# Attention with a gated convolution: periodic due times, row sums inverted in 128 rows, the last keys turned by VectorE, the low parts of the weights made by TensorE

## The chip, the cores and the metric

The kernel runs on one core of one Trainium2 chip. The metric is the device time of one execution in microseconds (us). The core has TensorE (PE; PEld is its weight load), VectorE (DVE), ScalarE (ACT), GpSimd (POOL) and SyncE (SP), which here only issues DMAs.

## The reference: what is computed

Inputs are q, k, v of shape (8 batches, 8 heads, 576 positions, 64), two 512x512 matrices `w_val` and `w_out`, and 5 convolution taps for each of 512 channels, these three as 64-bit floats.

```python
scores = scale * np.matmul(q_rot, k_rot.transpose(0, 1, 3, 2))
attn = np.exp(scores - np.max(scores, axis=-1, keepdims=True))
attn = attn / (np.sum(attn, axis=-1, keepdims=True) + 1e-09)
x = heads_joined(np.matmul(attn, v))            # (8, 576, 512)
gate_pre += conv_w[k][None, None, :] * xp[:, k:k + S, :]   # k = 0..4, causal
out = (1.0 / (1.0 + np.exp(-gate_pre)) * (x @ w_val)) @ w_out
```

`q_rot` and `k_rot` are q and k with rotary position embedding.

## The kernel before

**Pairs.** Two heads are worked on together, so there are 32 pairs (`p`), four to a batch. For a pair, q and k lie with 64 channels of each head on 128 partitions. One pair goes through these steps (names as in the code):

- `load`, `rope_mul`, `rope_add`, `qk_hi`, `qk_lo`: q and k come by DMA into one buffer each (`qin`, `kin`), are rotated, and split into a rounded high part (ACT) and a low part. Every score is the sum of three fp32r products, high x high, high x low, low x high.
- `s_mm`, `s_max`, `s_exp`: the 576 queries are taken in four chunks of 128 for each head, and the last 64 queries of both heads together (chunk 4). A chunk of 128 queries by 576 keys fills one of three PSUM tiles `ps_s`. DVE finds its maximum (L275), ACT takes the exponential (L288) and adds up the rows into a column of `sums`.
- Turning: for the product with v the keys must lie on partitions. For the first `EARLY` pairs and the last, TensorE transposes blocks of 128x128 through the identity (L318) into a bank of `ps_t`, of which there are two, and ACT or DVE copies it to `big` (`t_copy`). For all others, DVE transposes blocks of 32x32 (`turn`, L304) and 16 DMAs (`move`, L309) carry the blocks to their partitions. In both cases the last 64 keys of both heads are turned apart by TensorE (`th_mm`, L332, four transposes a pair) and copied to `pl` by ACT (`h_copy`).
- Sums: `hm_mm` turns the pair's nine columns of sums by TensorE into 16x128 (L362), `r_inv` adds 1e-9 and takes the reciprocal on DVE (L398, L399), `r_write` stores them in DRAM, and `r_read` reads them back, spread over 64 partitions.
- `pv_mm`, `pvm_mm`, `x_norm`, `xm_norm`: product with v, times the inverted sums.
- `x_hi`, `x_lo`, `tap`, `gate`: the result is split in high and low, and convolved (L446, four instructions on DVE, one on ACT).

After four pairs a batch is complete: `f_mm` (L472) multiplies by `w_val`, `y_mul`, `y_hi`, `y_lo` apply the gate and split, and `f_mm` multiplies by `w_out`; 16 groups of 12 matmuls a batch, dealt out between the matmuls of later pairs.

**Weights.** `load_weight` brings a 128x512 block of 64-bit numbers; DVE takes them apart with integer and float steps (`decode`, L506 to L512), ACT rounds to the high part (L517), and DVE subtracts it and adds the rest for the low part (L518, L519). There are eight blocks, all decoded during the first pairs.

**What sets the order.** Every step is a job with an engine, a cost, a due time (18 us times the pair, plus an offset, plus a number from the table `DUE`) and tokens that say what it reads and writes. `Plan.order` plays the jobs through with these costs: on each engine it starts, of the jobs that could begin within a short span, the one due first. What comes out is the order of instructions on each engine; engines then run in that order and wait for each other by semaphores. `PICK` says for jobs that several engines could do which one does them ('V' is DVE, 'A' ACT, 'G' POOL). SP's order is that of the DMAs, and a DMA that waits holds up all behind it.

## Time and profile before

| | |
|---|---|
| time, median of 3 runs | 727.49 us (727.17 to 730.32) |
| the profiled execution | 730.04 us, its span 728.2 us |
| TensorE clock granted, mean | 0.972 |
| PE busy | 653.0 us, 90% |
| DVE busy | 630.7 us, 87% |
| ACT busy | 464.7 us, 64% |
| POOL busy | 423.3 us, 58% |
| DMA queue of SP | 64.8% of 16 engines, 128.15 MB |

A matmul of fp32 operands shows as two instructions. The reciprocal of a pair's sums (L399) is a good mark of time, since there is one a pair: the one of pair 5 starts at 159.23 us, the one of pair 31 (the last) at 684.75 us. So the execution has an early stretch (0 to 159 us, with the weights), 26 steady pairs, and an end of 43 us.

### The profile page before, as it was taken

What the parts mean: (1) busy time and instruction counts of PE and PEld (TensorE: products, weight loads), DVE (VectorE), ACT (ScalarE), POOL (GpSimd) and SP (SyncE); (2) the same over time, 40 slices, a digit from 0 to 9 for tenths busy, and PEclk for the clock granted to TensorE, in tenths of its full rate; (3) what the DMA queues carried; (4) which work ended last, traced back from release to release, by engine and by line L of the source; (5) the groups of instructions that cost most, each with busy time, mean ns of one, the idle gap of its engine ahead of it and who ended that gap; (6) DMA issues with size and microseconds to landing.
All of it is one profiled execution on the core that took longest, in us unless ns stands there. A gap on an engine that the chain in (4) does not pass through costs nothing.

```text
span 728.2 us, 14173 instructions
## 1 busy us (share of the span) xinstructions
PE 653.0 (90%) x5044; PEld 473.2 (65%) x5044; DVE 630.7 (87%) x980; ACT 464.7 (64%) x1125; POOL 423.3 (58%) x312
## 2 busy tenths in 40 slices
PE   2787865799999989999899999999999899999998
PEld 2554552666666766777666666777665676777597
DVE  6999989999989998998889997889889899898452
ACT  3676564576776667676486666676686667776431
POOL 4474347278568775876657655777757555781000
PEclk9999878799999999999999999999999999999999
DMA  7245133558888787877976877878876868866101
GB/s 257 66 130 186 30 101 129 114 154 220 231 226 217 206 214 195 214 213 216 225 205 186 211 203 184 213 202 214 232 222 175 221 184 222 215 187 153 49 33 66
DMA packets 52245, 129.63 MB, mean 178 GB/s; under 512 B 11184, under 2 KB 21200, under 8 KB 52176
## 3 DMA queue, kind: packets, MB, share of 16 engines
q1 hardware_dynamic: 51632, 128.15, 64.8%
q8 instruction: 40, 0.66, 0.4%
q10 hardware_dynamic: 544, 0.59, 0.3%
q14 instruction: 29, 0.24, 0.1%
HBM read 62.48 MB, written 9.59 MB: 99 GB/s over the span
## 4 chain that ended last, share of the span: by engine, by line
PE 37%; DVE 31%; DMA 13%; ACT 6%; SPq 6%; issue 5%; POOL 2%; DVEq 0%; ACTq 0%; POOLq 0%
PE ps_t L472 13%; PE ps_t L377 9%; DVE nm L275 9%; PE ps_s L269 8%; DVE g L446 6%; DVE big L304 6%; SPq L309 4%; DMA kin<-in_k 4%; ACT p L288 3%; DMA v<-in_v 3%; DMA big<-big 3%; PE ps_t L380 3%; DMA rb<-rd 2%; DVE kin L233 2%; DVE rr L399 1%
## 5 line engine op out<-in xcount | busy, mean ns | idle before, releaser
L288 ACT ACTIVATE p<-ps_s,nm 128x576 f32<-128x576 f32 x256 | 188.1, 739 | 79.1 <-DVE nm L275 76.6
L275 DVE TENSOR_REDUCE nm<-ps_s 128x1 f32<-128x576 f32 x288 | 204.2, 738 | 23.4 <-PE ps_s L269 22.4
L269 PE MATMUL ps_s<-k,q 64*128 64x288 f32 x1536 | 152.0, 320 | 20.2 <-ACT k L244 8.9
L269 PEld LDWEIGHTS ps_s<-k,q 64*128 64x128 f32 x1536 | 116.6, 193 | 52.2 <-issue 21.0
L304 DVE STREAM_TRANSPOSE big<-p 128x512 f32<-128x512 f32 x216 | 142.4, 685 | 6.1 <-ACT p L288 5.9
L233 POOL TENSOR_TENSOR qin<-qin,tab 128x576 f32<-128x576 f32 x59 | 87.5, 1497 | 70.4 <-DMA qin<-in_q 64.3
L446 DVE SCALAR_TENSOR_TENSOR g<-x,cw,g 128x576 f32<-128x576 f32 (+1 forms) x132 | 125.6, 956 | 1.9 <-ACT g L443 1.7
L377 PE MATMUL ps_t<-big,v 128*64 128x512 f32 (+2 forms) x528 | 119.4, 586 | 5.5 <-DMA rd<-rr 3.2
L472 PE MATMUL ps_t<-yh,wout_hi 128*128 128x288 f32 x256 | 81.2, 317 | 4.9 <-ACT pl L213 1.8
L472 PE MATMUL ps_t<-xh,wval_hi 128*128 128x288 f32 x256 | 80.1, 313 | 3.1 <-DVE g L477 2.0
L237 POOL TENSOR_TENSOR kin<-kin 128x576 f32<-128x576 f32 (+1 forms) x32 | 51.0, 1594 | 45.9 <-DVE kin L233 38.8
L472 PE MATMUL ps_t<-yh,wout_lo 128*128 128x288 f32 x256 | 77.5, 303 | 0.0
L472 PE MATMUL ps_t<-yl,wout_hi 128*128 128x288 f32 x256 | 77.4, 302 | 0.0
L472 PE MATMUL ps_t<-xl,wval_hi 128*128 128x288 f32 x256 | 76.8, 300 | 0.0
L472 PE MATMUL ps_t<-xh,wval_lo 128*128 128x288 f32 x256 | 76.5, 299 | 0.0
L377 PEld LDWEIGHTS ps_t<-big,v 128*64 128x64 f32 x528 | 36.1, 136 | 62.1 <-issue 56.4
L433 POOL TENSOR_TENSOR xl<-x,xh 128x576 fp32r<-128x576 f32 (+1 forms) x32 | 51.5, 1608 | 41.6 <-ACT xh L429 39.9
L485 POOL TENSOR_TENSOR yl<-g,yh 128x288 fp32r<-128x288 f32 x56 | 47.2, 843 | 34.9 <-ACT yh L481 34.8
L248 POOL TENSOR_TENSOR q<-qin,q 128x576 fp32r<-128x576 f32 (+1 forms) x32 | 49.2, 1536 | 31.3 <-ACT q L244 31.3
L233 POOL TENSOR_TENSOR kin<-kin,tab 128x576 f32<-128x576 f32 x34 | 52.5, 1547 | 14.5 <-DMA kin<-in_k 14.5
L248 POOL TENSOR_TENSOR k<-kin,k 128x576 fp32r<-128x576 f32 x31 | 45.8, 1479 | 23.0 <-ACT k L244 21.9
L472 PEld LDWEIGHTS ps_t<-yh,wout_hi 128*128 128x128 f32 x256 | 49.2, 192 | 10.4 <-DVE g L477 2.6
(86 smaller groups left out, 1150.5 us busy)
## 6 DMA issues: line engine op xcount, KB each, us to landing
big<-big SPq DMA_DIRECT2D x432, 128.0 KB
kin<-in_k SPq DMA_DIRECT2D x31, 576.0 KB
qin<-in_q SPq DMA_DIRECT2D x31, 576.0 KB
v<-in_v SPq DMA_DIRECT2D x32, 320.0 KB
rb<-rd SPq DMA_DIRECT2D x64, 144.0 KB
out_t<-oo SPq DMA_DIRECT2D x64, 144.0 KB
big<-in_w_val SPq DMA_DIRECT2D x4, 512.0 KB
big<-in_w_out SPq DMA_DIRECT2D x4, 512.0 KB
```

The source lines that it names most:

```text
L233: eng.tensor_tensor(out=t[:, i, a:b], in0=t[:, i, a:b], in1=tabs[:, i, a:b], op=ALU.mult)
L237: eng.tensor_tensor(out=t[:, 0], in0=t[:, 0], in1=t[:, 1], op=ALU.add)
L248: eng.tensor_tensor(out=t[:, 1], in0=ins[n][:, 0, a:b], in1=t[:, 0].bitcast(F32), op=ALU.subtract)
L269: T.matmul(out=ps[:, half, 0:288], lhsT=st["q"][rows, x, c * 128:c * 128 + 128] if c < 4 else mixq[p % 2][:, x], rhs=st["k"][rows, y, k0:k ...
L275: V.tensor_reduce(out=st[f"nm{i}"], in_=st[f"s{i}"], axis=AX.XY, op=ALU.max, negate=True)
L288: A.activation(out=pd.rearrange("p (b x) -> p b x", b=2), in_=st[f"s{i}"], func=AF.Exp, bias=st[f"nm{i}"], scale=1.0, accum_out=sums[p % 2 ...
L304: V.transpose(out=t[:, :, cs.index(c), h].rearrange("p b k i -> p k b i"), in_=st[f"p{c}"][:, h, h * D:h * D + M].rearrange("p (k b i) -> ...
L377: T.matmul(out=acc[HEAD[h], 0:n], lhsT=st["v"][:, j, h, :], rhs=st["pt"][:, :, c0:c1, h, j].rearrange("p a c i -> p c a i"), start=(j == 0 ...
L433: eng.tensor_tensor(out=st["xl"][:, a:b], in0=xs[p % 2][:, 4 + a:4 + b], in1=st["xh"][:, a:b].bitcast(F32), op=ALU.subtract)
L446: V.scalar_tensor_tensor(out=g, in0=x_sb[:, a + k:b + k], scalar=w, in1=g, op0=ALU.mult, op1=ALU.add)
L472: T.matmul(out=acc[:, 0:n], lhsT=wt[w][:, kc, ds], rhs=mv, start=(kc == 0 and i == 0), stop=(kc == NCH - 1 and i == 2))
L485: eng.tensor_tensor(out=ffn[b, "l", dc, lo], in0=y, in1=ffn[b, "h", dc, lo].bitcast(F32), op=ALU.subtract)
```

## The change

- **Order.** `Plan.order` no longer plays costs through. It takes, among all jobs whose forerunners have been placed and whose buffers can be given, always the one due first. The due times have 18.5 us times the pair, and a new table `DUE` (the offset of `exp0`, for instance, goes from -341.33 to -875.49); `PICK` is new too. For the pairs after the early ones, `rope_mul` of k's first half goes from DVE to POOL (`kmul0` 'V' to 'G'), `hm_copy` from ACT to DVE (`chm`), and one in four `o_out` from ACT to DVE (`od1`). For the early pairs, POOL gives three rope steps of k to DVE and takes two of q.
- **Early pairs.** `EARLY` goes from 4 to 5: pair 4 is turned by TensorE.
- **Sums.** `r_inv` works on the sums as they lie, 9 columns in 128 rows, and writes them beside the exponentials of chunk 4 in `pm`, so that the transpose of the last 64 keys of `pm` turns them too. The transpose L362 is gone, and `r_write` now follows the copy `hm_copy`.
- **Last keys.** For pairs turned by DVE, `turn` of the second head takes five blocks of 128 keys and the other four, so that all 9 x 128 columns are turned; `th_mm` and `h_copy` remain for pairs turned by TensorE. Each `move` carries 144 KB and not 128 KB. `pl` is gone.
- **Weights.** One mask step of `decode` becomes an Abs on ACT; the subtraction and addition on DVE become three matmuls of 512 columns through the identity and its negative (`w_mm`) and a copy by ACT (`w_low`).
- Of the buffers `yh` and `yl` there are 7 and not 8.

```diff
-EARLY = 4
+EARLY = 5
...
-            "rb": 2, "rr": 1, "yl": 8, "oo": 3, "rd": 2, "ps_s": 3, "ps_t": 2, "nm": 4}
+    BUFS = {"p": 3, "pm": 1, "big": 3, "pq": 1, "xh": 5, "xl": 5, "g": 5, "yh": 7, "rb": 2, "yl": 7, "oo": 3, "rd": 2,
+            "ps_s": 3, "ps_t": 2, "nm": 4}
...
+        heap = [(jobs[i][0], i) for i in range(len(jobs)) if not left[i]]
+        heapify(heap)
         done = []
+        while heap:
+            i = heappop(heap)[1]
...
+                done.append(i)
+                for o in outs[i]:
+                    left[o] -= 1
+                    if not left[o]:
+                        heappush(heap, (jobs[o][0], o))
...
+        k0, k1 = ((0, 4), (4, 9))[h]
+        V.transpose(out=t[:, :, cs.index(c), k0:k1].rearrange("p b k i -> p k b i"),
+                    in_=st[f"p{c}"].rearrange("p h s -> p (h s)")[:, k0 * 128:k1 * 128].rearrange("p (k b i) -> p k b i", b=4, i=32))
...
-        T.transpose(out=st["bhm"][:, 0:128], in_=st["pm"][:, 448:S], identity=ident)
-        T.transpose(out=st["bhm"][0:16, 128:256], in_=sums[p % 2], identity=ident)
+        T.transpose(out=state[p]["bhm"][:, 0:128], in_=pm[:, M:S + D], identity=ident)
...
-        V.tensor_scalar(out=r, in0=st["bhm"][0:16, 128:256], scalar1=1e-9, scalar2=None, op0=ALU.add)
-        V.reciprocal(out=r, in_=r)
+        r = sums[p % 2][:, 0:9]
+        V.tensor_scalar(out=r, in0=r, scalar1=1e-9, scalar2=None, op0=ALU.add)
+        V.reciprocal(out=pm[:, S:S + 9], in_=r)
...
-            lambda: V.tensor_scalar(out=hi, in0=hi, scalar1=0x7FF00000, scalar2=None, op0=ALU.bitwise_and),
+            lambda: A.activation(out=fh, in_=fh, func=AF.Abs) if whole is None else
+            V.tensor_scalar(out=hi, in0=hi, scalar1=0x7FF00000, scalar2=None, op0=ALU.bitwise_and),
...
-            lambda: eng.tensor_tensor(out=fa, in0=fa, in1=hi_out.bitcast(F32), op=ALU.subtract),
-            lambda: eng.tensor_tensor(out=lo_out, in0=fa, in1=fh, op=ALU.add),
...
+    def w_mm(n, c):
+        _, fa, fh = wsteps[n, c]
+        b = wstage["lo", n, c] = bank(f"ps_t/w{n}{c}")
+        T.matmul(out=b, lhsT=minus, rhs=w_hi[n][:, c], start=True, stop=False)
+        T.matmul(out=b, lhsT=ident, rhs=fa, start=False, stop=False)
+        T.matmul(out=b, lhsT=ident, rhs=fh, start=False, stop=True)
+
+    def w_low(n, c, eng):
+        cast(eng, w_lo[n][:, c], wstage["lo", n, c])
```

**How the order moves.** First PE in pair 0: between the scores of chunks 1 and 3. Before (L269 are scores, L318 and L332 transposes of the exponentials `p`):

```order
L269 MATMUL ps_s_163<-k_70,q_72 128x288
L318 MATMUL ps_t_178<-ident,p_158 128x128 x4
L318 MATMUL ps_t_188<-ident,p_158 128x128 x4
L269 MATMUL ps_s_201<-k_70,q_72 128x288
L269 MATMUL ps_s_202<-k_70,q_72 128x288
```

With the change (L230 are scores, L280 a transpose, L506 to L508 the new matmuls for the first block of `w_val`):

```order
L230 MATMUL ps_s_193<-k_71,q_73 128x288
L280 MATMUL ps_t_206<-ident,p_190 128x128 x4
L506 MATMUL ps_t_220<-wval_hi,minus 128x512
L507 MATMUL ps_t_220<-big_118,ident 128x512
L508 MATMUL ps_t_220<-big_118,ident 128x512
L230 MATMUL ps_s_228<-k_71,q_73 128x288
L230 MATMUL ps_s_229<-k_71,q_73 128x288
```

The scores of chunk 3 now stand behind matmuls that need a decoded block.

Second, POOL in a steady pair. `qin`, `kin` are the two input buffers; L233 is `rope_mul`, L237 `rope_add`, L248 `qk_lo`, L433 `x_lo`. Before:

```order
L233 TENSOR_TENSOR kin<-kin,tab 128x576
L237 TENSOR_TENSOR kin<-kin 128x576
L233 TENSOR_TENSOR qin<-qin,tab 128x576 x2
L248 TENSOR_TENSOR k_71<-kin,k_71 128x576
L433 TENSOR_TENSOR xl_5351<-x_83,xh_5350 128x576
L237 TENSOR_TENSOR qin<-qin 128x576
L248 TENSOR_TENSOR q_73<-qin,q_73 128x576
```

With the change the same steps are L194, L198, L209 and L392:

```order
L194 TENSOR_TENSOR qin<-qin,tab 128x576 x2
L194 TENSOR_TENSOR kin<-kin,tab 128x576 x2
L198 TENSOR_TENSOR kin<-kin 128x576
L198 TENSOR_TENSOR qin<-qin 128x576
L209 TENSOR_TENSOR k_72<-kin,k_72 128x576
L209 TENSOR_TENSOR q_74<-qin,q_74 128x576
L392 TENSOR_TENSOR xl_6262<-x_86,xh_6261 128x576
```

All eight steps of q and k stand together on POOL, q's first step first and q's last step last.

Third, DVE around the inverted sums of a steady pair. L275 is a maximum, L304 a `turn`, L418 and L422 the products with the inverted sums, L446 a tap. Before:

```order
L304 STREAM_TRANSPOSE big_5101<-p_5230 128x4x4x32 x2
L233 TENSOR_TENSOR kin<-kin,tab 128x576
L422 TENSOR_TENSOR x_83<-ps_t_5186,rb_5198 128x64
L418 TENSOR_TENSOR x_83<-ps_t_5221,rb_5198 128x512
L275 TENSOR_REDUCE nm_5268<-ps_s_5251 128x1
L398 TENSOR_SCALAR rr_5310<-ps_t_5311 16x128
L399 RECIPROCAL rr_5310<-rr_5310 16x128
```

With the change (L236 a maximum, L266 a `turn`, L357 and L358 the inverted sums, L176 the copy `hm_copy`, L377 and L381 the products, L405 a tap):

```order
L405 SCALAR_TENSOR_TENSOR g_4927<-x_86,cw,g_4927 128x576
L377 TENSOR_TENSOR x_85<-ps_t_5037,rb_5070 128x512
L266 STREAM_TRANSPOSE big_5123<-p_5110 128x4x4x32
L236 TENSOR_REDUCE nm_5142<-ps_s_5128 128x1
L357 TENSOR_SCALAR sums_88<-sums_88 128x9
L358 RECIPROCAL pm<-sums_88 128x9
L381 TENSOR_TENSOR x_85<-ps_t_5148,rb_5070 128x64
L236 TENSOR_REDUCE nm_5162<-ps_s_5129 128x1
L266 STREAM_TRANSPOSE big_5123<-p_5110 128x5x4x32
L176 COPY pq_5182<-ps_t_5183 96x128
```

The rope step L233 has left DVE; the sums are inverted ahead of PE's transpose, and the copy of what it turned stands a few instructions behind.

More of the change, by code (lines that the diff above doesn't have):

```diff
@@ L45, in __init__, with add @@
     def __init__(self):
         self.jobs = []
-    def add(self, due, engine, ns, fn, *args, r="", w="", kb=0, mode=None, port=False, hold=False):
-        self.jobs.append((due, engine, ns, fn, args, r.split(), w.split(), kb * 3.6, mode, port or engine == "G", hold))
+    def add(self, due, engine, fn, *args, r="", w=""):
+        self.jobs.append((due, engine, fn, args, r.split(), w.split()))
     def graph(self):
@@ L161, in order @@
-        self.start, self.end = start, end
+                    idle = [(freed.get(held, -1), k) for k, held in enumerate(slots[tag])
+                            if (tag, k) not in [g[1:] for g in got] and not to_come.get(held)]
+                    if not idle:
+                        parked[tag].append(i)
+                        break
+                    got.append((inst, tag, min(idle)[1]))
+            else:
+                for inst, tag, k in got:
+                    self.slot[inst], self.before[inst] = k, slots[tag][k]
+                    slots[tag][k] = inst
+                for inst in uses[i]:
+                    to_come[inst] -= 1
+                    freed[inst] = len(done)
+                    if not to_come[inst]:
+                        tag = inst.split("/")[0]
+                        for j in parked[tag]:
+                            heappush(heap, (jobs[j][0], j))
+                        parked[tag] = []
+                done.append(i)
[3 more added lines that the diff above has]
+                        heappush(heap, (jobs[o][0], o))
@@ L162, in order @@
+        assert len(done) == len(jobs), "no job can start"
         return done
@@ L343, in tm_mm @@
         for j in range(4):
-            T.transpose(out=st["bm"][:, j * 128:(j + 1) * 128], in_=st["pm"][:, j * 128:(j + 1) * 128], identity=ident)
+            T.transpose(out=st["bm"][:, j * 128:(j + 1) * 128], in_=pm[:, j * 128:(j + 1) * 128], identity=ident)
     def mixed(p):
@@ L527, in load_taps @@
         tmp = get("oo/taps1", [128, G1])[:, 0:NCH * TAPS]
[L528 removed]
+        taps.extend(decode(st, tmp, whole=cw))
     wsteps, wstage = {}, {}
@@ L578, in attn_gated_ffn @@
     for i in range(7):
-        at("dtap", 16 + 0.4 * i, "V", 150, lambda i=i: taps[i](), w="cw oo/taps0 oo/taps1", port=i in (1, 3, 5, 6), hold=True)
+        at("dtap", 16 + 0.4 * i, "V", 150, lambda i=i: taps[i](), w="cw oo/taps0 oo/taps1", port=i in (1, 3, 5, 6))
     def weights(n):
```

214 lines of the change are left out of this document (74 added, 140 removed).

## The prediction

> **What bounds the kernel now.** I read the page first, then the busy time of each engine by stretches cut at the reciprocals of pairs 5 and 31, then the early stretch in pieces of 5 us.
>
> ```profile
> span 728.2 us, 14173 instructions
> PE 653.0 (90%) x5044; PEld 473.2 (65%) x5044; DVE 630.7 (87%) x980; ACT 464.7 (64%) x1125; POOL 423.3 (58%) x312
> ```
>
> ```profile
> 0.00:159.23 159.23, 114.60 (x794) 77.39 (x795) 142.93 (x223) 95.47 (x219) 82.08 (x60) 0.90 0.40 128
> 159.23:684.75 525.52, 498.46 (x3940) 359.49 (x3938) 470.22 (x721) 357.30 (x881) 339.46 (x252) 0.99 0.78 204
> 684.75:728.20 43.45, 39.91 (x312) 36.29 (x312) 17.55 (x36) 11.94 (x27) 1.77 (x2) 1.00 0.15 52
> ```
>
> The columns are the stretch, its length, busy time of PE, PEld, DVE, ACT and POOL, the granted clock, and the share and rate of DMA. In the 26 steady pairs PE is busy 498.46 of 525.52 us, 94.9%: 19.17 us a pair of 20.21. DVE has 18.09 us a pair (89.5%), POOL 13.06. So a steady pair costs what PE has to do plus 1.04 us, and DVE is close behind. In the early stretch it is the other way round: DVE 142.93 of 159.23 us, PE 114.60. The 75 us in which PE rests are 44.6 early, 27.1 in the 26 pairs, 3.5 at the end.
>
> ```profile
> 0.00:20.00 20.00, 6.65 (x33) 5.06 (x33) 12.96 (x27) 7.12 (x14) 9.51 (x14) 1.00 0.67 234
> ...
> 70.00:75.00 5.00, 3.07 (x16) 2.48 (x17) 5.00 (x6) 2.52 (x6) 3.55 (x2) 0.61 0.46 184
> ...
> 95.00:100.00 5.00, 2.50 (x9) 1.85 (x9) 5.00 (x11) 2.71 (x5) 1.77 (x1) 0.50 0.60 228
> 100.00:105.00 5.00, 4.50 (x23) 3.65 (x23) 3.10 (x6) 3.91 (x12) 5.00 (x2) 0.50 0.00 0
> ...
> 120.00:125.00 5.00, 0.00 (x0) 0.00 (x0) 5.00 (x4) 0.61 (x2) 4.83 (x3) 0.73 0.45 162
> ...
> 130.00:135.00 5.00, 4.05 (x21) 3.56 (x22) 4.67 (x8) 3.26 (x10) 0.00 (x0) 0.50 0.00 0
> ```
>
> ```profile
> PE ps_t L332 <- ACT p L288: 11.2, 1, 11.2
> ...
> PEld ps_t L377 <- issue: 56.4, 204, 1.5
> ```
>
> From 120 to 130 us PE does nothing while DVE is full: the list of waits names one rest of PE of 11.2 us, for exponentials that stand behind maxima, which stand behind weight steps on DVE. The clock is halved around such rests.
>
> **Steady pairs, PE.** Rows of the steady stretch alone, grouped by line:
>
> ```profile
> L332 PE MATMUL ps_t<-ident,p 128*128 128x128 f32 x104 | 22.5, 296 | 5.9 <-DVE x L422 4.7 <-DVE x L418 0.5 <-ACT oo L491 0.2
> L362 PE MATMUL ps_t<-ident,sums 128*16 128x128 f32 x26 | 7.2, 278 | 0.0
> ```
>
> Busy time over count is what one adds, since matmuls overlap: 22.5 us over 26 pairs is 0.87 a pair, 7.2 us is 0.28. Both go: -1.15. Against it, the new order changes between scores, value products and full matmuls once more a pair (the value product is split by scores); the waits for "issue" ahead of L377 in the list above, 56.4 us in 204 times, price one at 0.28, of which I take half, 0.15. PE then has 18.2 us a pair. If PE kept its 94.9% the pair would take 19.15.
>
> **Steady pairs, DVE.**
>
> ```profile
> L304 DVE STREAM_TRANSPOSE big<-p 128x512 f32<-128x512 f32 x200 | 132.0, 685 | 6.1 <-ACT p L288 5.9
> L399 DVE RECIPROCAL rr<-rr 16x128 f32<-16x128 f32 x26 | 24.5, 941 | 0.9
> L233 DVE TENSOR_TENSOR kin<-kin,tab 128x576 f32<-128x576 f32 x24 | 22.9, 956 | 3.5 <-DMA kin<-in_k 3.5
> L398 DVE TENSOR_SCALAR rr<-ps_t 16x128 f32<-16x128 f32 x26 | 7.1, 274 | 2.6 <-ACT pq L213 1.6 <-PE ps_t L362 0.5 <-DMA v<-in_v 0.3
> L422 DVE TENSOR_TENSOR x<-ps_t,rb 128x64 f32<-128x64 f32 x26 | 5.5, 213 | 11.7 <-DMA rb<-rd 8.2 <-PE ps_t L392 2.3 <-PE ps_t L380 1.1
> ```
>
> ```profile
> L215 DVE COPY pl<-ps_t 128x256 f32<-128x256 f32 x4 | 1.6, 412 | 1.4 <-PE ps_t L332 1.4
> L511 DVE TENSOR_SCALAR oo<-oo 128x20 int32<-128x20 int32 x1 | 0.2, 167 | 0.0
> ```
>
> The rope step leaves: -0.96. The inverted sums cost 0.274 + 0.941 = 1.215 now; in the new form each row holds 9 numbers instead of 128. No row has a reciprocal of 9; the row nearest in size is the 128x20 step at 167 ns, so two of them make 0.33, and the bounds are 0 and 1.215 (nothing won). I take 0.3: -0.92. Four `turn` of 640 columns instead of 512 add 4 x 0.685 x 128/512 = 0.69. `hm_copy` (96x128 from PSUM) lies between 0.213 and 0.412; I take 0.29. One `o_out` of 288 columns for every two pairs, 0.46 by the copy of 256, adds 0.23. The sum is -0.67: 17.4 us a pair, 90% of 19.4.
>
> **Steady pairs, POOL, ACT, DMA.** POOL takes the rope step at 1.49: 14.55 a pair. ACT's 357.30 us are 13.7 a pair, and it only loses work here (two copies of 256 columns, `hm_copy`, some `o_out`); it is never near the bound. The moves grow by 16 x 16 KB = 256 KB a pair; the 204 GB/s of the steady stretch over 20.21 us are 4.1 MB, so +6%: DMA's 0.78 x 20.21 = 15.8 us becomes 16.8, 87% of 19.4.
>
> **What could queue.** The input buffers are single, so a load waits until POOL has done its last step with them.
>
> ```profile
> L237 POOL TENSOR_TENSOR kin<-kin 128x576 f32<-128x576 f32 x25 | 39.9, 1596 | 26.1 <-DVE kin L233 19.2 <-DVE x L422 6.7
> L248 POOL TENSOR_TENSOR q<-qin,q 128x576 fp32r<-128x576 f32 x25 | 39.6, 1585 | 25.6 <-ACT q L244 25.6
> L237 POOL TENSOR_TENSOR qin<-qin 128x576 f32<-128x576 f32 x25 | 38.2, 1528 | 0.6
> L248 POOL TENSOR_TENSOR k<-kin,k 128x576 fp32r<-128x576 f32 x25 | 37.1, 1485 | 8.5 <-ACT k L244 7.5 <-DVE rr L398 0.9
> L233 POOL TENSOR_TENSOR kin<-kin,tab 128x576 f32<-128x576 f32 x24 | 35.7, 1486 | 10.2 <-DMA kin<-in_k 10.2
> ```
>
> ```profile
> 307.65 0.54 SPq L219 DMA_DIRECT2D qin<-in_q  x1
> 312.45 2.79 POOL L233 TENSOR_TENSOR qin<-qin,tab 128x576 f32<-128x576 f32 x2 [3.04 <-DMA qin<-in_q]
> ```
>
> With the change q's loop holds all eight steps: two each of 1.4 (q's rope, from the 2.79 for two) and 1.486, then 1.596, 1.528, 1.485 and 1.585, together 12.0 us, and a load of 4.8 us from issue to use (the two timeline rows). That is 16.8 us, 2.6 below a pair of 19.4, and `x_lo` and `y_lo` fit into the time of the load. The sums now pass DVE, PE, DVE and only then SP's `r_write`, with v, outputs and the read behind it on SP's queue; from PE's transpose to the product that needs the read there are some 10 us of other PE work, so I cost it at nothing. If that cover is gone, DVE waits longer than the 8.2 us in 26 pairs that L422's row now shows for this read (`rb<-rd`), and the next scores behind it.
>
> I take 19.4 us a pair, between PE's 19.15 and 17.4 / 0.895 = 19.5, which DVE would give at its present share. 26 x (20.21 - 19.4) = **-21 us**.
>
> **Early stretch.**
>
> ```profile
> L509 DVE TENSOR_SCALAR big<-big 128x512 int32<-128x512 int32 x8 | 3.5, 437 | 0.0
> L518 DVE TENSOR_TENSOR big<-big,wout_hi 128x512 f32<-128x512 f32 x4 | 3.9, 970 | 0.0
> L518 DVE TENSOR_TENSOR big<-big,wval_hi 128x512 f32<-128x512 f32 x4 | 3.2, 801 | 0.0
> L519 DVE TENSOR_TENSOR wval_lo<-big 128x512 fp32r<-128x512 f32 x4 | 3.9, 962 | 0.0
> L213 ACT COPY big<-ps_t 128x512 f32<-128x512 f32 x33 | 18.6, 588 | 11.6 <-PE ps_t L318 11.4
> L318 PE MATMUL ps_t<-ident,p 128*128 128x128 f32 x128 | 23.5, 333 | 10.0 <-DVE x L418 4.5 <-ACT big L213 2.4 <-DVE big L215 1.7
> ```
>
> ```profile
> 35.62 1.89 PE ps_t L377 x8
> ```
>
> DVE loses 0.437 + 0.885 + 0.96 a block, eight blocks, -18 us; the inverted sums of pairs 0 to 4, -4.6; pair 4's eight `turn`, -5.5. Rope gives it three steps a pair instead of two and takes them to about +3. So 143 becomes 118 us. ACT takes eight Abs and eight copies, 8 x 2 x 0.59 = +9.4, on 95. PE gets `w_mm`: eight column-tiled instructions of 512 columns take 1.89 us in the chain, four full-height fp32 products running two by two, so 0.93 for one of full width, two a block; the fp32r one adds about 0.27. That is 2.1 us x 8 = +17. The bounds are 1.0 (if a transposing weight went at the rate of L318) and 2.8 a block (at half clock for half of them). Pair 4's 32 transposes add 32 x 23.5/128 = +5.9, the sums give back 1.8, and one group of output matmuls less (1.8) stands ahead of pair 5's reciprocal. 114.6 becomes 134, less what a halved clock costs now: from the rows above, about 6 to 8 us (where the clock reads 0.50, half of PE's busy time), of which I credit half. So PE has some 130 us, DVE 118, and PE's rest of 44.6 us, of which the first 20 us hold 13, cannot go below that; I leave 23. The stretch ends at 153: **-6 us**. The rest of 11.2 us goes; what is late next is PE itself, which has the new matmuls in its queue and scores behind them that wait for a decoded block.
>
> The Trainium skill (TensorE: Matmul & The Clock Gate, "What's actually happening") says that one idle window of about 3.4 us halves PE's clock until it has been busy as long. The rows of 95 to 135 us agree: 0.50 around rests of 10 us. By that rule an early stretch without such rests runs at full clock, which is part of the first rival.
>
> **End.** The last batch's groups stand in another order: the second product of the second half now follows at once on the group whose gate, rounding and low part it needs, a chain of three steps of 288 columns (about 0.46 each on DVE and ACT, half of 1.5 on POOL, and the hops between): **+2 us**.
>
> **Sum.** -21 - 6 + 2 = -25 against the profiled execution's 730.0: 705. The three runs have a median 2.5 us below that execution, the fastest 2.9; I leave 705 as the forecast and put the difference into the range.
>
> **Rivals.** (1) *Both stretches gain fully.* PE's early rest shrinks to little more than the head and the clock stays up (-14), and the pair takes 19.1 (-29): with the end, 689. For it: DVE had the early stretch alone. Against: PE is in order and gets work that waits for DVE. (2) *DVE takes over.* Two engines above 90%, in order, wait for each other; if DVE can do no more than 88% with 17.4 to do, the pair takes 19.8, the sum is -11 - 6 + 2, 715. (3) *The reciprocal costs as much in the new form*, or DVE's work does not fall for another reason: 18.3 us at 89.5% makes 20.4, the steady gain is gone (+5), with -6 and +2 the time is about that of before, 730. Against: the reciprocal's 941 ns for 128 numbers a row point to a cost by column. (4) *The input loop binds*, the slower end. It decides from the point where load and waits exceed 20.2 - 12.0 = 8.2 us instead of 4.8. For it: POOL waited 64.3 us for q in 18 times and SP 32.0 us for POOL's last step with k, and loads took up to 7.7 us in the chain of waits:
>
> ```profile
> POOL qin L233 <- DMA qin<-in_q: 64.3, 18, 8.9
> SPq L219 <- POOL k L248: 32.0, 13, 14.0
> ```
>
> ```profile
> 571.43 7.70 DMA kin<-in_k
> ```
>
> ```profile
> L446 DVE SCALAR_TENSOR_TENSOR g<-x,cw,g x132: 509/809/2000, 48.3 to 696.0; 128x576 f32<-128x576 f32 x124, 128x288 f32<-128x288 f32 x8
> ```
>
> With 7.7 us and 1.2 of SP's queue the loop is 20.9: 26 x 0.7 = +18, with -6 and +2 the time is 744. Against it: in the new order the load stands right behind the moves, and 2.6 us are to spare. The taps spread from 0.5 to 2.0 us beside POOL's work, so POOL's extra step also costs DVE something, 0.1 to 0.2 us a pair by that spread. The Trainium skill (SBUF — State Buffer, "SBUF: two separate sides") gives the reason: DVE operations with two SBUF inputs and GpSimd ones take one port pair in turn, each blocking the other whole. The trace agrees; by that rule the move of the rope step to POOL speaks against the change, in the way of (2) and (4).
>
> **Chances.** The forecast, 696 to 722, has 0.50; (1) 0.10; (2) 0.14, much of it inside those bounds; (3) 0.09; (4) 0.17. About 0.5%, 3.6 us, is what a measurement of this kernel can tell from no change. Faster by more: forecast, (1) and (2), 0.74. Within it: (3), 0.09. Slower: (4), 0.17. The range runs from 689, the first rival, to 733, the near end of the fourth, and leaves out half of (1) and most of (4).
>
> **What the profile of the changed kernel would show.** PE busy near 644 us (653 + 17 + 6 - 32). The reciprocal of pair 5 near 153 us and 26 pairs of 19.4 from there. L358 far below 941 ns, near 0.15. POOL busy near 460 us, its waits for q not above 3 us a pair. PE without a rest of 10 us before the first output matmuls. Wrong would be: POOL or SP waiting more for the inputs, PE resting at L506 to L508 for over 2 us a block, or a DVE share above 93% with PE's below 92%.

## The result and the profile after

| | before | after |
|---|---|---|
| time, median | 727.58 us (727.17 to 730.32, 4 runs) | 702.12 us (697.72 to 707.72, 4 runs) |
| ratio | | 0.9647, 95% interval 0.9568 to 0.9725 |
| profiled execution, its span | 730.04, 728.2 us | 699.96, 698.1 us |
| TensorE clock granted, mean | 0.972 | 0.993 |

The change made the kernel faster, by 25.5 us; 705 was forecast. Ratios leave out runs over 1.5% above the fastest of the same kernel, medians hold all runs. First the page's head and the same three stretches as before (again cut at the reciprocals of pairs 5 and 31):

```profile
span 698.1 us, 13986 instructions
PE 636.8 (91%) x4980; PEld 456.4 (65%) x4980; DVE 608.2 (87%) x974; ACT 446.2 (64%) x1049; POOL 448.0 (64%) x334
```

```profile
0.00:151.50 151.50, 121.08 (x853) 78.50 (x853) 129.74 (x205) 106.28 (x236) 76.47 (x58) 0.98 0.37 124
151.50:647.05 495.55, 469.69 (x3761) 336.34 (x3762) 459.08 (x730) 324.84 (x781) 365.80 (x272) 1.00 0.87 228
647.05:698.10 51.05, 46.04 (x369) 41.57 (x367) 19.40 (x39) 15.07 (x33) 5.69 (x5) 1.00 0.14 47
```

The early stretch ends 7.7 us sooner, the 26 steady pairs are 30.0 us shorter, the end is 7.6 us longer: -30.1 us of span. That is more than the 25.5 us between the medians, for the profiled execution was the slowest of four before and the second fastest of four now. In the steady pairs PE is busy 28.8 us less, and its rest went from 27.1 to 25.9 us.

A part of these figures is only a shift of the mark. The reciprocal now stands earlier in a pair, ahead of output matmuls: those before pair 5's mark held PE for 12.4 us and now for 9.2, those behind pair 31's for 32.4 and now for 37.4 (all of L472 and L431). So here is a second cut, at the product of chunk 4 with the inverted sums of the same two pairs, before (L422) and with the change (L381):

```profile
176.03 0.23 DVE L422 TENSOR_TENSOR x<-ps_t,rb 128x64 f32<-128x64 f32 x1 [1.13 <-PE ps_t L380]
692.60 0.23 DVE L422 TENSOR_TENSOR x<-ps_t,rb 128x64 f32<-128x64 f32 x1 [0.16 <-PE ps_t L392]
```

```profile
171.32 0.16 DVE L381 TENSOR_TENSOR x<-ps_t,rb 128x64 f32<-128x64 f32 x1
661.08 0.23 DVE L381 TENSOR_TENSOR x<-ps_t,rb 128x64 f32<-128x64 f32 x1 [0.58 <-PE ps_t L352]
```

By it the three are -4.7, -26.8 and +1.4 us. By either cut the gain is in the steady pairs.

The groups of DVE in the steady stretch (L266 is `turn`, L357 and L358 the inverted sums, L405 the taps):

```profile
L405 DVE SCALAR_TENSOR_TENSOR g<-x,cw,g 128x576 f32<-128x576 f32 x102 | 103.2, 1012 | 0.0
L266 DVE STREAM_TRANSPOSE big<-p 128x640 f32<-128x640 f32 x100 | 82.1, 821 | 0.0
L357 DVE TENSOR_SCALAR sums<-sums 128x9 f32<-128x9 f32 x26 | 20.4, 784 | 0.0
L358 DVE RECIPROCAL pm<-sums 128x9 f32<-128x9 f32 x26 | 5.6, 216 | 0.9
```

The reciprocal is cheap, as expected. The addition of 1e-9 to the same nine numbers, before it, takes 784 ns on average and is the surprise of this profile.

The waits of the whole execution (engine and line, what it waited for, us, times, longest):

```profile
POOL qin L194 <- DMA qin<-in_q: 69.4, 22, 6.0
...
PE ps_s L230 <- ACT q L205: 11.2, 1, 11.2
...
DVE x L377 <- DMA rb<-rd: 9.8, 8, 2.9
...
POOL kin L194 <- DMA kin<-in_k: 6.0, 6, 2.0
```

The one rest of PE over 10 us is the start, for the first q. The rest of 11.2 us in the middle of the weights is gone.

The new matmuls of the weights (L506 to L508), one block of the eight, from the timeline (start, length):

```profile
46.06 0.50 PE L506 MATMUL ps_t<-wval_hi,minus 128*128 128x512 f32 x1
46.40 1.02 PE L507 MATMUL ps_t<-big,ident 128*128 128x512 f32 x2
47.26 1.06 PE L508 MATMUL ps_t<-big,ident 128*128 128x512 f32 x2
48.16 0.38 PE L293 MATMUL ps_t<-ident,p 128*128 128x128 f32 x2
```

From its first start to its last end the block takes 2.26 us; the eight take 2.25 to 2.54 us each, 18.4 us together, and PE never rested ahead of them.

### The profile page after: what moved, and what is told of

It reads as the page before. It is cut to its first block, busy times and chain, and to the rows that moved or that the text cites. A ratio compares the mean times of both kernels' runs of the same rounds, so it can differ in the third digit from the quotient of the medians.

```text
span 698.1 us, 13986 instructions
## 1 busy us (share of the span) xinstructions
PE 636.8 (91%) x4980; PEld 456.4 (65%) x4980; DVE 608.2 (87%) x974; ACT 446.2 (64%) x1049; POOL 448.0 (64%) x334
## 4 chain that ended last, share of the span: by engine, by line
PE 48%; DVE 26%; DMA 15%; SPq 4%; issue 3%; ACT 3%; POOL 1%; DVEq 0%; POOLq 0%; ACTq 0%
PE ps_t L431 19%; PE ps_s L230 11%; PE ps_t L337 9%; DVE nm L236 7%; DVE big L266 6%; DVE g L405 5%; DMA big<-big 5%; DMA v<-in_v 4%; SPq L271 3%; PE ps_t L340 2%; PE ps_t L280 2%; DMA rb<-rd 2%; DMA rd<-pq 2%; DVE sums L357 2%; DMA kin<-in_k 2%
## 5 line engine op out<-in xcount | busy, mean ns | idle before, releaser
L236 DVE TENSOR_REDUCE nm<-ps_s 128x1 f32<-128x576 f32 x288 | 203.6, 740 | 14.8 <-PE ps_s L230 14.6
L230 PE MATMUL ps_s<-k,q 64*128 64x288 f32 x1536 | 142.9, 314 | 17.2 <-ACT q L205 11.2
L266 DVE STREAM_TRANSPOSE big<-p 128x512 f32<-128x512 f32 (+1 forms) x208 | 150.9, 754 | 0.0
L230 PEld LDWEIGHTS ps_s<-k,q 64*128 64x128 f32 x1536 | 110.6, 188 | 60.7 <-ACT p L249 20.3
L194 POOL TENSOR_TENSOR qin<-qin,tab 128x576 f32<-128x576 f32 x62 | 91.9, 1500 | 73.7 <-DMA qin<-in_q 69.4
L405 DVE SCALAR_TENSOR_TENSOR g<-x,cw,g 128x576 f32<-128x576 f32 (+1 forms) x132 | 131.1, 993 | 0.2
L337 PE MATMUL ps_t<-big,v 128*64 128x512 f32 (+2 forms) x528 | 122.5, 590 | 4.9 <-issue 1.9
L194 POOL TENSOR_TENSOR kin<-kin,tab 128x576 f32<-128x576 f32 (+1 forms) x56 | 83.8, 1517 | 10.0 <-DMA kin<-in_k 6.0
L392 POOL TENSOR_TENSOR xl<-x,xh 128x576 fp32r<-128x576 f32 (+1 forms) x33 | 46.7, 1422 | 58.9 <-ACT xh L388 58.9
L431 PE MATMUL ps_t<-yh,wout_hi 128*128 128x288 f32 x256 | 80.3, 313 | 4.6 <-DVE x L377 2.3
L209 POOL TENSOR_TENSOR q<-qin,q 128x576 fp32r<-128x576 f32 (+1 forms) x32 | 48.8, 1524 | 53.4 <-ACT q L205 50.8
L431 PE MATMUL ps_t<-xh,wval_hi 128*128 128x288 f32 x256 | 78.9, 308 | 2.3 <-DVE x L381 1.0
L431 PE MATMUL ps_t<-yl,wout_hi 128*128 128x288 f32 x256 | 76.5, 299 | 0.1
L431 PE MATMUL ps_t<-yh,wout_lo 128*128 128x288 f32 x256 | 76.0, 297 | 0.0
L431 PE MATMUL ps_t<-xh,wval_lo 128*128 128x288 f32 x256 | 75.4, 295 | 0.0
L431 PE MATMUL ps_t<-xl,wval_hi 128*128 128x288 f32 x256 | 75.3, 294 | 0.0
L337 PEld LDWEIGHTS ps_t<-big,v 128*64 128x64 f32 x528 | 33.6, 136 | 55.5 <-issue 48.2
L431 PEld LDWEIGHTS ps_t<-yh,wout_hi 128*128 128x128 f32 x256 | 48.7, 190 | 15.5 <-issue 4.9
L431 PEld LDWEIGHTS ps_t<-xh,wval_hi 128*128 128x128 f32 x256 | 48.1, 188 | 11.0 <-ACT p L249 4.9
L209 POOL TENSOR_TENSOR k<-kin,k 128x576 fp32r<-128x576 f32 x31 | 44.3, 1428 | 11.2 <-ACT k L205 11.2
```

The lines of the kernel that those rows point to most:

```text
L194: eng.tensor_tensor(out=t[:, i, a:b], in0=t[:, i, a:b], in1=tabs[:, i, a:b], op=ALU.mult)
L209: eng.tensor_tensor(out=t[:, 1], in0=ins[n][:, 0, a:b], in1=t[:, 0].bitcast(F32), op=ALU.subtract)
L230: T.matmul(out=ps[:, half, 0:288], lhsT=st["q"][rows, x, c * 128:c * 128 + 128] if c < 4 else mixq[p % 2][:, x], rhs=st["k"][rows, y, k0:k ...
L236: V.tensor_reduce(out=st[f"nm{i}"], in_=st[f"s{i}"], axis=AX.XY, op=ALU.max, negate=True)
L266: V.transpose(out=t[:, :, cs.index(c), k0:k1].rearrange("p b k i -> p k b i"), in_=st[f"p{c}"].rearrange("p h s -> p (h s)")[:, k0 * 128:k ...
L337: T.matmul(out=acc[HEAD[h], 0:n], lhsT=st["v"][:, j, h, :], rhs=st["pt"][:, :, c0:c1, 5 * h + j].rearrange("p a c i -> p c a i"), start=(j ...
```

## Experiments

The theory at the start: a steady pair is set by PE with DVE close behind, the early stretch by DVE; each part of the change takes work off one of the two. Differences between two variants are given as differences of their ratios to the kernel before, with the two half-widths added in squares; 0.01 of a ratio is 7.3 us. Such an interval holds the spread of the runs. The variants were run in three sets, each on one chip, together with the kernel before, whose median was 727.5 us in set A, 728.7 in B and 726.0 in C.

### The addition left out (set A)

```diff
-        V.tensor_scalar(out=r, in0=r, scalar1=1e-9, scalar2=None, op0=ALU.add)
         V.reciprocal(out=pm[:, S:S + 9], in_=r)
```

> The changed kernel without the addition of 1e-9 to the sums (L357). Every sum is at least 1, since the largest exponential of a row is exp(0), so in fp32 the addition changes nothing; it is left out here as a cost. In the changed kernel it takes 784 ns a pair in the steady stretch, for 9 numbers a row, against 216 ns of the reciprocal behind it. Theory (DVE, 17.66 us of a pair of 19.06, is a second bound beside PE): DVE falls to about 16.9 a pair, the pair to 18.7 to 18.9, the time by 4 to 9 us from 702, to 693 to 698. Rival (PE or the DMAs set the pair alone): within 2 us of 702.

Measured 696.32 us (692.30 to 702.72), ratio 0.9547 (0.9495 to 0.9598). The steady stretch:

```profile
148.87:646.19 497.32, 472.26 (x3769) 339.98 (x3768) 448.22 (x705) 321.66 (x782) 367.65 (x274) 0.99 0.86 228
```

L357's 20.4 us in this stretch are gone, but DVE's busy time fell by only 10.9 (459.08 to 448.22), and in the profiled execution the stretch did not get shorter. What the addition waited for POOL inside its own busy time, other instructions then waited for: the same 102 taps took 111.5 us here and 103.2 after the change, and DVE's waits for the read of the sums (`rb<-rd`, L376 here) rose from 9.8 to 13.8 us. The median lies where the theory had it, 693 to 698, 7.3 +- 6.8 us below the change; the last part of this section tells what is left of that.

### The sums inverted as before (set A)

```diff
-        r = sums[p % 2][:, 0:9]
-        V.tensor_scalar(out=r, in0=r, scalar1=1e-9, scalar2=None, op0=ALU.add)
-        V.reciprocal(out=pm[:, S:S + 9], in_=r)
+        V.tensor_scalar(out=r, in0=st["bhm"][0:16, 128:256], scalar1=1e-9, scalar2=None, op0=ALU.add)
+        V.reciprocal(out=r, in_=r)
```

with the transpose of the sums on PE again.

> The changed kernel with one part undone: sums turned by TensorE into 16 x 128 and inverted there on DVE, as before. PE gets 0.28 us a pair more, DVE 1.215 instead of 1.0. Theory (PE bound, DVE close behind): the pair grows by 0.3 to 0.4, the time to 709 to 713. Rival (this part was worth a whole microsecond a pair, as the prediction had it for DVE alone, through something the DVE row does not show, the longer path of the sums among it): outside 706 to 718, below where the longer path costs, above where the old form does.

Measured 710.04 us (707.86 to 712.12), ratio 0.9738 (0.9678 to 0.9798): as expected, 6.6 +- 7.1 us above the change, so by itself hardly more than its uncertainty. In the same set it lies 13.9 +- 5.8 us above the kernel without the addition. The steady stretch:

```profile
155.30:663.72 508.42, 483.52 (x3821) 346.06 (x3817) 458.73 (x729) 321.76 (x780) 372.16 (x271) 0.99 0.84 222
```

DVE is as busy as after the change (458.73, and 459.08 there): what the cheap reciprocal saves, the addition beside POOL takes back. PE has 13.8 us more in this stretch and the stretch is 12.9 us longer, but the mark has moved back here. Over the whole execution PE is busy 11.8 us more; the 32 transposes of the sums take 9.1 us as a group, and the scores, the same 1728 instructions, 5.0 us more than after the change. The span is 12.3 us longer in this execution, which is the slowest of its four. By the trace this part of the change acts through PE, hardly through DVE; by the medians its worth is not clear of zero.

### The weights as before (set A)

```diff
-            lambda: A.activation(out=fh, in_=fh, func=AF.Abs) if whole is None else
+            lambda: V.tensor_scalar(out=hi, in0=hi, scalar1=0x7FF00000, scalar2=None, op0=ALU.bitwise_and),
...
+            lambda: V.tensor_tensor(out=fa, in0=fa, in1=hi_out.bitcast(F32), op=ALU.subtract),
+            lambda: V.tensor_tensor(out=lo_out, in0=fa, in1=fh, op=ALU.add),
```

> The changed kernel with one part undone: the low parts of the weights by DVE again (mask, subtraction and addition; no matmuls through the identity). In the early stretch DVE's 130 us become 148, PE's 121 become 104, and ACT loses 9. Theory (DVE set the early stretch): the reciprocal of pair 5, now at 151.5 us, comes at 162 to 168, the time at 712 to 719. Rival (the early stretch is set by the chain of pairs and PE's order, and the work only changed its engine): the reciprocal of pair 5 within 4 us of 151.5, the time within 4 us of 702.

Measured 718.07 us (713.36 to 720.44), ratio 0.9850 (0.9794 to 0.9906), 14.8 +- 7.0 us above the change, where the theory had it. In the profiled execution, whose span is 18.7 us longer, 14.8 of them are in the early stretch:

```profile
0.00:166.30 166.30, 120.69 (x813) 83.00 (x813) 145.39 (x229) 97.40 (x220) 79.25 (x58) 0.87 0.34 113
166.30:665.76 499.46, 474.43 (x3763) 339.33 (x3762) 462.87 (x730) 325.18 (x781) 365.57 (x272) 0.99 0.86 227
```

PE does 40 instructions fewer here than after the change and is busy just as long (120.69 and 121.08 us), at a clock of 0.87 against 0.98. So the 18.4 us of new matmuls did not show in PE's busy time: with them PE rests 30.4 us in this stretch and not 45.6, and the clock granted is the higher one. The early stretch is also 7 us longer here than in the kernel before (159.23): the other parts of the change, pair 4 on TensorE among them, cost it about that much, and the new form of the weights more than pays for them.

### The last keys turned by PE, as before (sets A and B)

```diff
-        k0, k1 = ((0, 4), (4, 9))[h]
-        V.transpose(out=t[:, :, cs.index(c), k0:k1].rearrange("p b k i -> p k b i"),
+        V.transpose(out=t[:, :, cs.index(c), h].rearrange("p b k i -> p k b i"),
...
-            cl = tuple(c for c in cl if c not in cs)
-            if cl:
+            if True:
```

The transposes got due times of their own (`th1` 14.5, `th3` 17.7), and both copies are on ACT, at the due times that the new table had for the early pairs.

> The changed kernel with one part undone: the last 64 keys of all pairs are turned by TensorE again (four transposes a pair), copied by ACT, and the DVE transposes have 512 columns and the moves 128 KB again. PE gets 0.87 us a pair more (18.07 becomes 18.9), DVE 0.55 less (17.66 becomes 17.1), the DMAs 6% less. Theory (PE's work sets the pair): at PE's 94.8% the pair takes 19.9 to 20.0, 26 x 0.9 = +23: 720 to 727. Rival (DVE or the DMAs set it): 695 to 704.

Measured 779.61 us (772.75 to 789.24), ratio 1.0671 (1.0600 to 1.0743): a miss by 50 us. The waits show ACT waiting, in its order, for the transposes:

```profile
ACT big L174 <- PE ps_t L294: 99.6, 29, 5.9
```

So the copies were put later in ACT's order (`ch1` due at 15.6, `ch3` at 18.0), in set B:

> As x2 (the last 64 keys of all pairs turned by TensorE and copied by ACT again), but ACT's copies stand two or three exponentials later in ACT's order. In x2 ACT waited 99.6 us for the transposes, with exponentials queued behind. If that misplaced wait made x2's time, it falls to what PE's work gives: PE 0.9 us a pair more, 720 to 727. If the two banks of ps_t, which the transposes hold until they are copied, are the cause, it stays above 745. Rival of the first study (DVE or the DMAs set the pair): 695 to 704.

Measured 758.29 us (757.91 to 760.21), ratio 1.0439 (1.0393 to 1.0486). A miss again, on the side named for the two banks of `ps_t`:

```profile
DVE nm L236 <- PE ps_s L230: 61.7, 36, 4.8
PE ps_t L431 <- ACT big L174: 25.4, 17, 3.6
```

PE waits 25.4 us for ACT to empty a bank, and DVE for the scores behind it. This part cannot be priced alone: in a table made for the new work, the old form of it costs far more than in the kernel before, which had it.

### More work for PE (set B)

The four transposes of chunk 4 (`tm`, L307) are done twice in every pair.

```diff
-        for j in range(4):
+        for j in (0, 1, 2, 3, 0, 1, 2, 3):
```

> The changed kernel with TensorE's four transposes of pm done twice in every pair, into the same bank with the same result: 4 x 0.16 = 0.66 us of PE more a pair by the row of these transposes, no other engine's work touched, no new buffer. Theory (PE's work sets the pair): 28 to 32 pairs x 0.66, divided by nothing as PE does not wait more: +18 to +22, 719 to 725. Rival (PE has slack that another engine sets): below 710.

Measured 711.34 us (708.38 to 711.84), ratio 0.9779 (0.9732 to 0.9827): 9.6 +- 6.6 us more.

```profile
L307 PE MATMUL ps_t<-ident,pm 128*128 128x128 f32 x256 | 35.8, 284 | 1.2 <-DVE pq L176 1.0 <-ACT big L174 0.2
```

The group was 21.0 us for 128, so it grew by 14.8, and PE's busy time by 18.3. About half comes through, between 3 and 16 us by the interval.

### More work for DVE (set B)

One of the eight `turn` of a pair is repeated in the 26 pairs turned by DVE.

```diff
-        V.transpose(out=t[:, :, cs.index(c), k0:k1].rearrange("p b k i -> p k b i"),
-                    in_=...)
+        for _ in range(2 if i == 2 else 1):
+            V.transpose(out=t[:, :, cs.index(c), k0:k1].rearrange("p b k i -> p k b i"),
+                        in_=...)
```

> The changed kernel with one of DVE's eight transposes a pair done twice (chunk 1 of the first head, 512 columns, 0.685 us), same result, in the 26 pairs that DVE turns: DVE goes from 17.66 to 18.35 us a pair. Theory (PE sets the pair, DVE at 93% is close behind and passes on a part): +4 to +10, 706 to 712. Rival A (PE alone): within 3 us of 702. Rival B (DVE is the bound now): 26 x 0.69 = +18, above 717.

Measured 713.70 us (712.02 to 715.69), ratio 0.9821 (0.9773 to 0.9870): 12.7 +- 6.7 us more, for 26 repeats at 690 ns, 17.9 us. About two thirds come through, between the two expectations; by the interval it could be a third or all. With the run before: PE alone does not set the pair, and work added to either engine, each above 92% busy in its order, comes through in good part.

### The rope step back on DVE (set B)

```diff
-'kmul0': 'G'
+'kmul0': 'V'
```

> The changed kernel with the rope step of k (kmul0, pairs 5 to 31) back on DVE, all else the same: POOL 1.55 us a pair less (14.07 becomes 12.5), DVE 0.95 more (17.66 becomes 18.6). Theory (DVE is close behind PE): +6 to +18, 708 to 720. Rival (POOL, its port shared with DVE, and the input loop set the pair): faster than 699.

Measured 851.17 us (844.40 to 856.13), ratio 1.1695 (1.1592 to 1.1798): both theories missed, by over 130 us.

```profile
PE ps_s L230 <- ACT p L249: 113.8, 26, 7.7
DVE kin L194 <- DMA kin<-in_k: 103.3, 24, 6.8
```

At its due time the step waits for k's load, 4.3 us a pair; on POOL that wait cost little, on DVE the maxima stand behind it, behind them the exponentials, and behind these PE. The step's 0.96 us say nothing of what it costs there.

### The new work in the order of before (set C)

The new work, with the old `Plan.order` and its costs, the old `DUE` and `PICK`, and 18 us a pair.

```diff
-        heap = [(jobs[i][0], i) for i in range(len(jobs)) if not left[i]]
-        heapify(heap)
+        ready = [1000 * due[i] if jobs[i][10] else 0.0 for i in range(n)]
+        free = dict.fromkeys(self.LAG, 0.0)
...
-    'exp0': -875.49
+    'exp0': -341.33
```

> The changed work (sums inverted in 128 rows, last keys turned by DVE, low parts of the weights summed on PE) issued by the planner of before: its costs, due times, choice of engines and period of 18; the multiplication kmul0 goes back to DVE with it. Theory (the work lays the bound lower, and the order of before fits the small edits): DVE's and PE's busy time fall by what the edits take away, less kmul0, which stays on DVE, and the time comes to 700 to 718 us, clearly under before. Rival (the gain is mostly that of the new order; the work alone was not what held a pair back): 720 us or more, near before.

Measured 750.66 us (749.15 to 756.05), ratio 1.0379 (1.0322 to 1.0437): the rival's side, and further, slower than the kernel before.

```profile
158.04:693.77 535.73, 488.36 (x3795) 351.69 (x3795) 471.76 (x721) 337.34 (x824) 326.98 (x245) 0.98 0.82 210
```

```profile
DVE nm L278 <- PE ps_s L272: 32.8, 35, 4.7
...
PE ps_s L272 <- ACT p L291: 17.9, 24, 2.8
DVE big L308 <- ACT p L291: 17.1, 27, 2.2
```

PE has 18.78 us a pair to do, less than the 19.17 of before, and the pair takes 20.61, more than the 20.21 of before. DVE's waits for scores (22.4 us before) and for exponentials ahead of a `turn` (5.9), and PE's for exponentials ahead of scores (8.7), have grown. DVE has as much to do as before (471.76 and 470.22 us), since the rope step stays on it by the old `PICK`. So less work on PE alone, in a table of due times made for the old steps, wins nothing. What the new order is worth by itself this run does not show: like the runs with a part undone, it pairs a table with work that it was not made for. The old work in the new order was not run whole; the last keys above are the nearest to it, and slower too.

### More work for POOL (set C)

```diff
-        eng.tensor_tensor(out=st["xl"][:, a:b], in0=..., op=ALU.subtract)
+        for _ in range(2 if EARLY <= p < 31 else 1):
+            eng.tensor_tensor(out=st["xl"][:, a:b], in0=..., op=ALU.subtract)
```

> The subtraction that makes the low part of x (POOL, 1.43 us) is done twice, with the same operands, in the 26 pairs 5 to 30; nothing else differs from the changed kernel. POOL's busy time rises by about 26 * 1.43 = 37 us. Theory (POOL has about 5 us of rest in a pair of 19.06 and is not the bound): the time rises by at most 6 us, to 708 or less. Rival (POOL, or the input loop that runs through it, or its hold on DVE's port sets the pair): most of the 37 us are passed on, 725 us or more; in between if it is the port that is shared: about half of what DVE then waits, 710 to 720.

Measured 719.18 us (713.32 to 723.82, 10 runs; the profiled one is the fastest), ratio 0.9915 (0.9879 to 0.9950): 19.5 +- 6.2 us more, for 41 us more of POOL's busy time in the steady stretch. The case between the two theories, the shared port, gave 710 to 720. The stretch, and from it the taps and POOL's first steps with q:

```profile
149.54:658.75 509.21, 476.31 (x3769) 341.37 (x3768) 469.36 (x730) 322.77 (x782) 406.75 (x297) 0.99 0.85 223
```

```profile
L406 DVE SCALAR_TENSOR_TENSOR g<-x,cw,g 128x576 f32<-128x576 f32 x102 | 117.6, 1153 | 4.8 <-ACT g L403 4.0 <-POOL yl L445 0.8
...
L194 POOL TENSOR_TENSOR qin<-qin,tab 128x576 f32<-128x576 f32 x48 | 69.8, 1475 | 31.8 <-DMA qin<-in_q 31.8
```

After the change the same taps took 103.2 us and POOL waited 55.3 us ahead of q's steps in this stretch. So 23.5 of the 41 us went into POOL's own rest; and the taps on DVE, the same 102 instructions on the same data, became 14.4 us longer. The input loop did not bind. That the taps wait for POOL shows in the changed kernel already: of its 124 taps of 576 columns, the 79 that start inside a step of POOL take 1149 ns on average, the other 45 take 805. So POOL has room, and still its work is not free. That these 14.4 us are what made the time longer fits, but no run took them apart from the later start of POOL's other steps (ACT's waits for k's sum, L198, went from 26.2 to 41.7 us).

### Can it be faster still (set C)

The kernel without the addition, with two output blocks of the very end exchanged:

```diff
-    'f0l4': 1713.68, 'f0l7': 1130.42
+    'f0l4': 1100.0, 'f0l7': 1713.0
```

> The kernel without the addition of 1e-9 to the sums (left out: the sums are 1 or more, where the addition changes nothing in single precision), and with the last batch's output blocks of one half in another order at the very end (the block whose data come first goes ahead of the one whose data come last). Theory (a pair is set by PE and DVE together, the end by PE's last blocks): the same as without the addition, less 0 to 1.2 us at the end: 692 to 697. Rival (the end gains nothing, and the lower time without the addition was the spread of the runs): 699 to 704.

Measured 699.29 us (693.04 to 703.01), ratio 0.9643 (0.9588 to 0.9698). The expected gain at the end is not there (52.36 us behind the last mark, and 51.21 without the exchange), and neither is the lower time of the kernel without the addition: 0.3 +- 6.9 us below the change. Its steady stretch:

```profile
149.68:645.34 495.66, 472.29 (x3769) 339.48 (x3768) 443.14 (x706) 321.19 (x782) 369.27 (x274) 0.99 0.87 229
```

DVE is 15.9 us less busy than after the change and the stretch is as long, 495.66 and 495.55 us. DVE's waits for the scores went from 6.6 to 11.1 us and those for the read of the sums from 9.8 to 15.4. So whether the addition costs any time stays open: one set says 7 us, the other nothing, and the rest of 52 us that DVE has here is no gain for PE. And on top of this one, `hm_copy` moved from DVE to ACT (`chm` from 'V' to 'A'):

> The same kernel as the one without the addition and with the end's blocks turned, and in it the copy of the middle keys' transposes (chm, 0.26 us a pair) moved from DVE to ACT, whose busy time is 446 of 698 us. Theory (DVE passes on about two thirds of what it is given or relieved of): 26 * 0.26 * 2/3 = 4 to 5 us less, 688 to 693. Rival (ACT takes it in its order, where it waits for PE's transposes as it did with the last keys on ACT): slower than without it, 700 us or more.

Measured 705.72 us (697.46 to 706.17), ratio 0.9719 (0.9656 to 0.9781): no gain, 5.5 +- 6.1 us above the kernel it was made from. DVE's steady busy time fell by 2.7 us instead of 6.8:

```profile
149.56:643.23 493.67, 470.10 (x3769) 336.97 (x3768) 440.49 (x679) 326.49 (x808) 369.24 (x274) 1.00 0.88 230
```

Neither theory is shown by it. No version here is reliably faster than the changed kernel.

## Why the prediction was right

The time and the sign were right, and so was the main path: a steady pair lost what PE lost. The three stretches came out as -7.7, -30.0 and +7.6 us by the mark, or -4.7, -26.8 and +1.4 by the products, where -6, -21 and +2 were forecast. So the steady pairs won 6 to 9 us more than forecast, and that the sum is close is partly luck. The steps that failed are named below. The runs spread more than the prediction allowed: 0.5% was to be told from no change, and the ratio's interval is 0.8% on either side.

- **PE in a steady pair.** 18.2 us forecast, 469.69 / 26 = 18.07 measured, and 94.8% busy where 94.9% was carried over. This step carried the forecast. Its 0.15 for one more change between kinds of matmul did not show: the waits for "issue" ahead of the value products went from 56.4 us in 204 times to 48.2 in 185.
- **DVE in a steady pair.** 17.4 forecast, 17.66 measured. The mis-sized term is the inverted sums: 0.3 us taken, 0.784 + 0.216 = 1.0 measured, near the upper bound of 1.215. The reciprocal was near its size; the price of the addition was read from a 128x20 step at 167 ns that ran where POOL did not hold it up. Two steps of the same size and operation stood in the same profile of before, in its early stretch, and would have warned; both started inside a step of POOL and ended 0.03 to 0.04 us behind it:

```profile
L506 DVE TENSOR_SCALAR oo<-oo 128x20 int32<-128x20 int32 x1 | 1.4, 1372 | 0.0
L509 DVE TENSOR_SCALAR oo<-oo 128x20 int32<-128x20 int32 x1 | 0.8, 761 | 0.0
```

  `turn` gave part of it back: 821 - 685 = 136 ns for the added block, 0.54 a pair and not 0.69. L381 also took 164 ns where L422 had taken 213.
- **The pair.** 19.4 us forecast, 495.55 / 26 = 19.06 measured: 26 x 0.34 = 9 us of the difference. The step that failed is the bound from DVE, 17.4 us at its share of then, 89.5%. With 17.66 us that would be 19.7; DVE's share rose to 92.6% instead. A share of busy time was no limit of the engine: part of DVE's busy time is waiting for POOL, and without the addition the stretch was as long with 11 to 16 us less of it. PE's side alone (19.15 at 94.9%) was the better forecast, and is the first rival's steady half. That the two engines are close to each other held: the two runs with added work gave on about half of PE's and two thirds of DVE's, within wide intervals.
- **POOL and the input loop.** 14.55 forecast, 365.80 / 26 = 14.07 measured; the waits for q are 69.4 us where they were 64.3, and for k 6.0 where they were 14.5. The loop did not bind, as forecast, and it still did not with 41 us more on POOL. One sign that was to count against the forecast came all the same: SP waited 68.8 us for POOL's last steps with q and k, and 49.8 before (32.0 of them for k). The waits of SP, before and with the change:

```profile
SPq L219 <- POOL q L248: 17.8, 15, 3.7
```

```profile
SPq L180 <- POOL q L209: 46.7, 9, 10.6
...
SPq L180 <- POOL k L209: 22.1, 3, 9.6
```

  It cost nothing that shows: POOL's waits for the two inputs were 75.4 us together, and 78.8 before. The cost beside POOL is real, though: 0.1 to 0.2 us a pair was forecast for the moved step; the taps grew from 973 to 1012 ns, 0.15 us for four, and the addition's 0.6 us above its undisturbed 0.16 was not in the sum.
- **The sums' longer way** was costed at nothing: DVE's waits for `rb` are 9.8 us (L377), before 8.2 + 3.9 for the two products. It held, with less room: SP waits 53.4 us for the store of the sums (L373), 13.7 before (L414).
- **Early stretch.** 153 forecast, 151.5 measured, and this is luck: two errors cancel. PE was busy 121.1 us, not 130. Output matmuls of 3.2 us, not 1.8, left the stretch with the mark; pair 5's transposes of the last keys left it too, which the sum had not counted (6.3 us for 24 before, 4.6 for 20); `w_mm` took 2.3 us a block, not 2.1, whose term of 0.27 had no row of its own. What is left of the difference, some 7 us, lies in work that stayed and got cheaper: the scores took 39.1 us for 348 instructions and 42.9 for 336 before, a transpose (L280, L318 before) 0.157 us by busy time over count and 0.184 before. The clock's rise from 0.90 to 0.98 fits that, where the sum had credited half of its cost; no run takes it apart. Against that, PE's rest was 30.4 us, not 23, for DVE had 129.7 us, not 118. The steps taken away were sized rightly; left out were the addition (3.3 us), casts and copies that moved to DVE (6.7 us became 9.6), three maxima and two taps more ahead of the mark, and that some steps which stay take longer beside POOL. The first weight step, from the groups of the early stretch, before and after:

```profile
L506 DVE TENSOR_SCALAR big<-big 128x512 int32<-128x512 int32 x8 | 3.4, 422 | 0.0
```

```profile
L465 DVE TENSOR_SCALAR big<-big 128x512 int32<-128x512 int32 x8 | 5.8, 728 | 0.0
```

  The clock read 0.50 again at 120 us, though the rest of 11.2 us was gone and the rests there are short. The stretch in pieces, and PE's steps behind these rests:

```profile
115.00:120.00 5.00, 2.93 (x16) 1.59 (x14) 4.97 (x7) 4.29 (x9) 3.56 (x3) 0.97 0.73 285
120.00:125.00 5.00, 3.21 (x18) 2.46 (x18) 3.33 (x4) 2.61 (x7) 4.92 (x4) 0.50 0.00 0
```

```profile
118.30 1.13 PE L280 MATMUL ps_t<-ident,p 128*128 128x128 f32 x8 [1.50 <-ACT p L249]
120.11 0.69 PE L293 MATMUL ps_t<-ident,p 128*128 128x128 f32 x2 [0.68 <-ACT big L174]
122.48 1.11 PE L280 MATMUL ps_t<-ident,p 128*128 128x128 f32 x4 [1.69 <-DVE big L176]
```

  The clock was halved from 119.7 us on, after rests of 1.5 and 0.7 us, with PE busy 1.6 of the 3.4 us before. So a window without any work, as in the rule that the prediction quotes, was not needed here. Also, the record of the clock begins at 24.1 us (26.7 before); its 1.00 up to there is no measurement, for the scores take 494 ns each from 20 to 22 us and 289 from 26 to 28.
- **End.** +2 forecast, +1.4 by the products; PE's rest there grew by 1.5 us.
- **The rivals.** The steady half of (1) came true, its early half did not. Of (2), DVE weighs about as much as PE, but its share had no ceiling at 88%. (3) was right that the sums hardly get cheaper (1.0 us of 1.215), through the addition and not the reciprocal; but DVE's work fell to 17.66 us and not to 18.3, and the steady gain stayed. (4) did not happen. That the order might matter was no rival, and the run with the order of before says it should have been one: nearly the same work came out at 750.66 us, above the upper end of the range.
- **What stays open.** The new form of the weights is worth 14.8 +- 7.0 us and the new form of the sums 6.6 +- 7.1. The last keys, the rope step and the order, which stand behind most of the steady gain, could not be priced one by one.

## What to carry to other kernels

Price a small instruction by rows that ran beside the same neighbours, not by rows of the same size elsewhere: 147 to 1383 ns for nine numbers. Where two engines were each above 90% busy in a fixed order, a microsecond added to one of them cost about half to two thirds of a microsecond, within wide intervals; taking away busy time that was only waiting inside an instruction gained nothing that two runs agree on. Busy times of groups that run into each other do not add up: count from a first start to a last end. A change of work and the order made for it belong together: undoing a part, or moving one step to another engine, in a table made for something else can cost far more than the step.
